# One piece of weights with each of the first four blocks, and the first three FFN products in halves of 256 columns

## The chip, the cores and the metric

The kernel runs on one core of a Trainium2 chip. The metric is the device time of one execution in microseconds (us). Of the core's engines, five matter here: TensorE (PE, matrix products and transposes; PEld is its loading of the stationary operand), VectorE (DVE), ScalarE (ACT), GpSimd (POOL), and SyncE (SP), whose queue issues nearly all DMAs. All arithmetic is in float32; the FFN's weights arrive as float64 and are converted on the chip.

## The reference

A retention attention over 8 batches of 8 heads, 576 positions, head size 64, is followed by a maxout feed-forward network (FFN) over the 4608 resulting rows of 512:

```
scores = q @ k.T / sqrt(64)                      # per batch and head
D[h, i, j] = gamma[h] ** (i - j) if i >= j else 0
attn = (scores * D) @ v                          # (8, 8, 576, 64) -> x (4608, 512)
h = max(max(x @ w1, x @ w2), x @ w3)             # w1, w2, w3: 512 x 768
out = h @ w_out                                  # w_out: 768 x 512
```

## The kernel before

**Tiles.** The 4608 rows are cut into blocks of 128 (`C`) and tiles of 512 (`NT`, so four blocks, `CPT`). The FFN works on a whole tile: `ffn(t)` for tile t, while the attention of tile t+1 is worked in between (`steps`, L1058). Only tile 0 has no earlier FFN to lie beside: its four blocks are worked ahead of and inside the first products. That opening is what the change touches.

**A block's attention.** `load(g)` (L248) issues the DMAs of k, q and v of block g on SP's queue, 256 KB each. `transposes` (L278) turns k and q on TensorE into PSUM, and ScalarE copies each out (`kT`, `qT`, L299). `scores(g)` (L301) makes the score products (L313, tile s) and their mask on VectorE (L336), and returns a function `state` that makes the key-value sums (L318, in the same PSUM tiles as the scores) and the running state on VectorE (L344 to L350). The key-value sums need v scaled by `decay` (L264): on GpSimd for blocks 1 and 2, on VectorE for blocks 0 and 3. `values([g])` (L429) makes masked scores times v (L454) and adds the part of the older state (L445); one-column copies called `first` on VectorE (L458) stand between. It returns a function, called `output` where it is used, that adds the second part and writes x, transposed, to `xT` on VectorE (L224).

**The FFN's products.** A unit is a pair of column blocks `fb` of one weight matrix `i`; `w(i, fb)` is one piece of weights, 512 x 128 float64 values, 512 KB, loaded by `load_weights` (L535) with two DMAs. `up_plain(t, h, fb, i, *parts)` (L870) makes one product of 512 columns in PSUM (four steps of depth 128), in parts if `parts` names ends: the first part is issued at once, and functions for the others and for the last step are returned. The last step is a ScalarE copy for i = 0 (L882) and a VectorE maximum otherwise (L880). Units 0 to 2 are i = 0, 1, 2 for `fb` 0 and 1.

**Conversion.** `convert_all` (L701) is one list of steps, taken a few at a time by `convert(n)` (L819). A piece goes through: exponent (VectorE L717, ScalarE `mant` L719), fraction (ScalarE L725, VectorE L726, ScalarE L728), whole (VectorE L731), sign and product (VectorE L735, L743, the converted piece w). The first six pieces go singly, later ones in pairs. After a product, the next piece not yet loaded is loaded.

**Order.** Each engine's instructions stand in the order of the program text, written out by hand, so where a `convert` stands decides what waits behind what on VectorE and ScalarE. `warm(n, ident)` (L173) issues n matmuls of 128 columns that compute nothing that is used. PSUM has three rings of buffers: `ps_r` (four), `ps_x` and `ps_y` (two each); a buffer is taken again when its last readers are through. The opening's order stands in L1010 to L1056 and goes on in `first_ups` (L889), which `ffn(0)` calls for unit 0.

Of the kernel before, what the change touches and what calls it, by code (L numbers as in the profile page):

```python
# [98 lines left out]
def kernel(  # L99
# [329 lines left out]
    def values(chunks):  # L429
        chore(len(urgent))  # L430
        t, i = divmod(chunks[0], CPT)
        return (chunk_values if chunks[0] >= BY_CHUNKS else parity_values)(chunks, t, i)

    def parity_values(chunks, t, i):
        pool, tag = (ps_r, "r") if chunks[0] >= CPT - 1 else (ps_y, "y")
        o = [pool.tile([P, len(chunks), NP, D], FP32, tag=tag, name="o") for _ in range(2)]
        cross = ((0, 0), (1, 1), (0, 1), (1, 0))

        def old(n):
            for b, g in enumerate(chunks):  # L440
                for u in range(0, NP, 2):
                    for j, c in cross:
                        m = j ^ n
                        if place(g, m) > 0:
                            nc.tensor.matmul(o[m][half(c), b, u + j, :],  # L445
                                             lhsT=(mids if m else states)[g][half(j), head(c, u) // 2, :],
                                             rhs=qks[g]["q"][half(j), head(c, u) // 2, half(m)],
                                             start=False, stop=True, skip_group_check=True)

        for b, g in enumerate(chunks):  # L450
            for u in range(NP):
                for m, c in cross:
                    h = head(c, u)
                    nc.tensor.matmul(o[m][half(c), b, u, :], lhsT=vds[g][half(m), h, :], rhs=sts[g][half(m), h, :],  # L454
                                     start=b == 0 and u == 0, stop=place(g, m) == 0, skip_group_check=True)
        old(0)
        for m in range(2):
            (nc.vector.tensor_copy if t == 0 else nc.scalar.copy)(first[:], o[m][:, 0, 0, 0:1])  # L458

        def rest():  # L460
            old(1)
            if t == 0:
                chunk_output(o, chunks, t, i)
            else:
                between.append(partial(chunk_output, o, chunks, t, i))

        if t == 0:
            return rest
        between.append(rest)
# [349 lines left out]
    def convert(n):  # L819
        for _ in range(n):  # L820
            next(converting, None)
# [67 lines left out]
    def first_ups(h):  # L889

        g = CPT - 1
        rest0, last0, copy0 = up_plain(0, h, 0, 0, 2 * C, g * C)
        transposes(g, "k")
        state()
        output = values([2])
        transposes(g, "q")
        convert(1)
        output()
        convert(1)
        following = scores(g)  # L900
        rest0()
        last1, copy1 = up_plain(0, h, 1, 0, g * C)
        convert(2)
        decay(g)
        following()
        output = values([g])
        convert(1)
        output()
        convert(1)
        for step in (last0, copy0, last1, copy1):  # L910
            step()
        convert(6)

    def ffn(t):

        h = hpool.tile([P, NF, NT], FP32, tag="h", name="h")
        if t == 0:
            a, b, c, d = range(CPT, 2 * CPT)
            middles = {units[2]: [(transposes, a)], units[3]: [(scores, a)], units[5]: [(scores, b)],
                       units[8]: [(scores, c, d)]}  # L920
            for fp, i in units:
                if (fp, i) == units[0]:
                    first_ups(h)
                    yield
                    continue
                for fb in (2 * fp, 2 * fp + 1):
                    maximum, = up_plain(t, h, fb, i)
                    if (fp, i) == units[-1] and fb % 2:
                        maximum()
                        convert(2)  # L930
                    else:
                        convert(4 if (fp, i) == units[1] else 2)
                        maximum()
                    for step, *blocks in middles.get((fp, i), ()) if fb == 2 * fp else ():
                        for g in blocks:
                            step(g)
                    scale(3)
                    if between:
                        between.pop()()
                yield  # L940
            convert(3)
            for fb, _ in enumerate(downs_plain(t, h, range(NF // 2))):
                convert(4 * len(pieces) if fb else 2)
                scale(4)
                if fb == 1:
                    while_converting.close()
                    late["pool"] = ctx.enter_context(tc.tile_pool(name="late", bufs=1))
                    state_factors()
                    nc.gpsimd.tensor_copy(causal[half(1), 0:D], causal[half(1), half(1)])
                    late_room()  # L950
                    weight_sums(0)
                if fb == 2:
                    between.pop()()
                chore((0, 2, 6, 6, len(chores), 0)[fb])
                if fb == 3:
                    between.pop()()
                if fb in (1, 3):
                    yield
            yield
            return  # L960
        order = (0, 2, 1)
        if t == 1:
            spread.append(True)
            weight_sums(2)
            weight_sums(1)
            form_groups = seven_forms(order)
        if t == 2:
            out_sums(order)
        total = len(order) * 2 * len(PRODUCTS)
        count = parts = 0  # L970
        for fp in order:
            while fp not in summed_fp:
                chore()
            for step, _ in enumerate(up(t, h, fp)):
                if step % 4 == 1 or step % 4 == 3 and len(urgent) > (2 if t == 1 else 6):
                    chore(len(urgent) > 0)
                elif chores:
                    chores.popleft()()
                if step % 3 == 2:
                    scale()  # L980
                if t == 1 and fp == order[-1] and step == 19:
                    chores.extend(form_groups[0])
                count += 1
                if count * (NF // 2 * 3) >= (parts + 1) * total:
                    parts += 1
                    yield
            if t == 1:
                seven_hidden(h, fp)
            elif fp != order[-1]:
                chores.extend(sums_of_hidden(h, order, 3 - order.index(fp)))  # L990
        chore(len(urgent) + len(chores))
        if t == 1:
            for n, _ in enumerate(downs_seven(t, order)):
                if n == 0:
                    for step in form_groups[1]:
                        step()
                chore(4)
                scale(2)
                if n in (1, 3):
                    yield  # L1000
        else:
            for n, _ in enumerate(downs(t, h, order)):
                chore(2)
                scale()
                if n in (3, 9):
                    yield
        yield


    warm(6)  # L1010
    load(0)
    load(1)
    load_weights(1)
    load(2, "kq")
    load_weights(1)
    load(2, "v")
    load(CPT - 1, "kq")
    load_weights(1)
    load(CPT - 1, "v")
    load_weights(1)  # L1020
    load_weights(2)
    for b in range(2):
        nc.vector.transpose(columns[b], rows[b])
        for c in range(2):
            shape = [D, 2, 4, 32]
            nc.vector.tensor_copy(
                factors[half(c)].rearrange("p (u b j) s -> p u b j s", b=2, j=4)[:, :, b],
                columns[b][half(c), 8 * c:8 * c + 8].rearrange("p (u j) -> p u j", j=4).unsqueeze(3).to_broadcast(shape))
# [3 lines left out]
    transposes(0)  # L1032
    warm(2)
    decay(1)
    state = scores(0)
    transposes(1, "k")
    state()
    transposes(1, "q")
    output = values([0])
    state = scores(1)  # L1040
    output()
    state()
    convert(2)
    warm(3, ident)
    output = values([1])
    warm(3, ident)
    output()
    transposes(2, "k")
    convert(1)
    warm(2, ident)  # L1050
    transposes(2, "q")
    convert(1)
    decay(2)
    warm(4, ident)
    state = scores(2)
    convert(2)  # L1056

    def steps(t):  # L1058

# [97 lines left out]
```

## Time and profile before

| what | value |
|---|---|
| median of 3 runs (lowest, highest) | 747.76 us (746.92, 749.10) |
| the profiled execution: its own time | 747.25 us |
| its span, first to last instruction | 745.5 us |
| TensorE busy in the span | 736.0 us, 99% |
| VectorE, ScalarE, GpSimd busy | 578.5, 344.8, 34.5 us |
| granted TensorE clock, mean | 0.999 |
| DMA over the span, mean | 79 GB/s |

Of the 40 slices of 18.6 us into which the page cuts the span, the first four move 214 to 263 GB/s: the opening is also when DMA is busiest. In the rows of a timeline the first number is the start in us from the span's start, the second the length in us, then engine, source line, operation, tile written <- tiles read, sizes and count; the bracket gives the idle time ahead of it and what ended that. A count of a product is in records: eight for the four steps of one product or part of it.

### The profile page before, as it was taken

The page shows a single profiled execution, that of the slowest core. Times are in us where ns is not written, and L with a number is a line of the kernel's source. Part 1 is how long each engine was busy: PE and PEld are TensorE (multiplying, and loading weights), DVE is VectorE, ACT ScalarE, POOL GpSimd, SP SyncE. Part 2 cuts the span into 40 slices and gives each one's busy share as a digit, 9 for nine tenths or more (in the row PEclk, how much of TensorE's full clock was granted, in tenths as well). Part 3 has the DMA queues.
Part 4 walks back from the last instruction along what each step waited for, and adds up shares of the span by engine and source line. Part 5 has one row for each costly group of instructions (what it writes and reads, how often), then busy time and mean ns, then how long its engine had stood idle before and what let it go on. Part 6 is the DMA issues. An engine that isn't in the chain of part 4 may idle for free.

```text
span 745.5 us, 17909 instructions
## 1 busy us (share of the span) xinstructions
PE 736.0 (99%) x7236; PEld 608.0 (82%) x7236; DVE 578.5 (78%) x1081; ACT 344.8 (46%) x731; POOL 34.5 (5%) x40
## 2 busy tenths in 40 slices
PE   8899999999999999999999999999999999999998
PEld 7645555888888888888888888888888888888887
DVE  6699898899886996588668877688668956893676
ACT  4376643555245443545354435552455345424441
POOL 1000000022000000000000001000100010000000
PEclk9999999999999999999999999999999999999999
DMA  9999352504242515242433234141514150001001
GB/s 214 237 234 263 91 99 65 93 18 83 72 88 46 92 35 114 44 77 46 95 70 63 53 71 100 30 87 46 119 27 95 39 113 22 3 23 35 0 1 58
DMA packets 226644, 58.91 MB, mean 79 GB/s; under 512 B 207872, under 2 KB 225280, under 8 KB 226560
## 3 DMA queue, kind: packets, MB, share of 16 engines
q1 hardware_dynamic: 225584, 57.71, 35.7%
q8 instruction: 57, 0.93, 0.5%
q14 instruction: 27, 0.22, 0.1%
q10 hardware_dynamic: 976, 0.04, 0.1%
HBM read 48.27 MB, written 9.44 MB: 77 GB/s over the span
## 4 chain that ended last, share of the span: by engine, by line
PE 95%; DVE 2%; DMA 1%; issue 1%; SPq 0%; ACT 0%; POOL 0%; DVEq 0%
PE a L850 19%; PE b L850 17%; PE c L850 9%; PE up L875 7%; PE di L694 6%; PE d L850 6%; PE e L850 6%; PE dhc L694 5%; PE deg L694 3%; PE sk L386 3%; PE down L862 3%; PE o L481 2%; PE dfd L694 2%; PE o L488 2%; PE dx L601 1%; PE kv L389 1%
## 5 line engine op out<-in xcount | busy, mean ns | idle before, releaser
L838 DVE TENSOR_TENSOR part<-part 128x512 f32<-128x512 f32 x168 | 117.9, 702 | 86.5 <-ACT part L835 83.9
L835 ACT COPY part<-b 128x512 f32<-128x512 f32 x120 | 70.3, 586 | 163.4 <-PE b L850 161.4
L838 DVE TENSOR_TENSOR h<-h,part 128x512 f32<-128x512 f32 x120 | 83.3, 694 | 24.5 <-ACT h L835 20.5
L835 ACT COPY part<-a 128x512 f32<-128x512 f32 x96 | 56.3, 586 | 50.7 <-PE a L850 50.2
L212 ACT ACTIVATE vraw<-vraw,gk 128x64 f32<-128x64 f32 x240 | 76.8, 347 | 0.9 <-DMA vraw<-in_v_dram 0.8
L850 PE MATMUL b<-s,n 128*128 128x256 f32 x288 | 73.9, 379 | 0.0
L875 PE MATMUL up<-xT,w 128*128 128x512 f32 (+3 forms) x168 | 65.1, 538 | 2.3 <-DVE w L743 1.4
L850 PEld LDWEIGHTS b<-s,n 128*128 128x128 f32 x288 | 54.7, 190 | 7.4
L875 PEld LDWEIGHTS up<-xT,w 128*128 128x128 f32 x168 | 29.1, 190 | 31.5 <-issue 25.5
L850 PE MATMUL c<-xT,w 128*128 128x256 f32 x192 | 51.2, 389 | 0.0
L683 ACT COPY k<-di 128x256 f32<-128x256 f32 x49 | 18.2, 372 | 68.5 <-PE di L694 43.4
L850 PE MATMUL d<-s,w 128*128 128x256 f32 x192 | 49.8, 380 | 0.0
L850 PE MATMUL b<-xT,n 128*128 128x256 f32 x192 | 49.3, 379 | 0.0
L850 PE MATMUL a<-s,w 128*128 128x256 f32 x192 | 49.3, 379 | 0.0
L850 PE MATMUL a<-xT,w 128*128 128x256 f32 x192 | 49.3, 379 | 0.0
L403 POOL TENSOR_TENSOR s<-s,gs_of 64x512 f32<-64x512 f32 x21 | 22.5, 1071 | 568.7 <-DVE s L401 534.7
L850 PE MATMUL a<-xT,n 128*128 128x256 f32 x192 | 45.4, 379 | 0.0
L850 PE MATMUL e<-xT,w 128*128 128x256 f32 x192 | 45.4, 379 | 0.0
L850 PEld LDWEIGHTS e<-xT,w 128*128 128x128 f32 x192 | 36.5, 190 | 5.4 <-issue 0.5
L850 PEld LDWEIGHTS a<-xT,w 128*128 128x128 f32 x192 | 36.5, 190 | 5.0
L850 PEld LDWEIGHTS a<-s,w 128*128 128x128 f32 x192 | 36.5, 190 | 5.0
L850 PEld LDWEIGHTS b<-xT,n 128*128 128x128 f32 x192 | 36.5, 190 | 5.0
(191 smaller groups left out, 1385.3 us busy)
## 6 DMA issues: line engine op xcount, KB each, us to landing
bits<-in_moe_w_dram SPq DMA_DIRECT2D x36, 256.0 KB, 5.5
kraw<-in_k_dram SPq DMA_DIRECT2D x32, 256.0 KB, 3.2
vraw<-in_v_dram SPq DMA_DIRECT2D x32, 256.0 KB, 3.6
qraw<-in_q_dram SPq DMA_DIRECT2D x224, 32.0 KB, 2.1
kxraw<-in_k_dram SPq DMA_DIRECT2D x224, 32.0 KB, 2.1
out_dram<-osb SPq DMA_DIRECT2D x56, 128.0 KB, 1.7
bits<-in_moe_w_out_dram SPq DMA_DIRECT2D x6, 512.0 KB, 5.8
qraw<-in_q_dram SPq DMA_DIRECT2D x7, 256.0 KB, 5.7
```

Source lines behind the costliest of these rows:

```text
L212: scaling.popleft()()
L386: nc.tensor.matmul(s[half(c), h, :], lhsT=kT[half(c), h, :], rhs=qT[half(c), h, :], start=True, stop=True)
L403: nc.gpsimd.tensor_tensor(new, new, factor, op=ALU.mult)
L481: nc.tensor.matmul(o[m][half(c), n, u, :], lhsT=vds[g][half(m), h, :], rhs=sts[g][half(m), h, :], start=n == 0 and u == 0, stop=place(g, m ...
L488: nc.tensor.matmul(o[m][half(c), n, u, :], lhsT=stacks[g][half(m), h, :], rhs=qks[g]["q"][half(m), h, :], start=False, stop=True, skip_gro ...
L683: nc.scalar.copy(place, a)
L694: nc.tensor.matmul(banks[chain], lhsT=hidden(h, order, b, late_ones)[:, e], rhs=late["V"][v][:, e], start=begins and e == 0, stop=chain no ...
L835: nc.scalar.copy(of[step], ps[step[0]][:])
L838: nc.vector.tensor_tensor(of[dst], a, b, op=op)
L850: nc.tensor.matmul(ps[chain][:, e, :], lhsT=factor(w, 2 * fp + e), rhs=xS[t][x], start=n == 1 and e == 0, stop=ends, skip_group_check=True)
L862: nc.tensor.matmul(b[:], lhsT=h[:, fb, m * P:(m + 1) * P], rhs=w_sb["out", fb], start=fb == blocks[0], stop=fb == blocks[-1])
L875: nc.tensor.matmul(ps[:, a:b], lhsT=w_sb[i, fb][:, dc * P:(dc + 1) * P], rhs=xT[t][:, dc, a:b], start=dc == 0 and a == 0, stop=dc == NDC - ...
```

## The change

Three things are different in the opening; nothing is changed from unit 1's second product on.

- Loads: one piece of weights is loaded behind each of blocks 0 to 3, and two more at the end. Before, pieces stood behind block 1, inside block 2's loads, inside block 3's and after them.
- The order of the opening: the scores and the key-value sums of blocks 0 and 1 are issued together; block 2's transposes stand at the end of the opening and its scores in `first_ups`; the idle `warm` matmuls with `ident` are 21 where they were 12.
- The first three products (w(0, 0), w(0, 1), w(1, 0)) are each made in two halves of 256 columns: the first halves between the attention of blocks 2 and 3, the second halves after block 3. Before, the first was made in 256 + 128 + 128 columns, the second in 384 + 128, and the third whole in `ffn`, which now skips it. The values of block 2 take their buffers from `ps_r`, not `ps_y`.

```diff
-        pool, tag = (ps_r, "r") if chunks[0] >= CPT - 1 else (ps_y, "y")
+        pool, tag = (ps_r, "r") if chunks[0] >= CPT - 2 else (ps_y, "y")
...
     def first_ups(h):
         g = CPT - 1
-        rest0, last0, copy0 = up_plain(0, h, 0, 0, 2 * C, g * C)
+        rest0, copy0 = up_plain(0, h, 0, 0, 2 * C)
+        convert(1)
+        state = scores(g - 1)
+        convert(1)
+        state()
+        rest1, copy1 = up_plain(0, h, 1, 0, 2 * C)
+        output = values([g - 1])
         transposes(g, "k")
+        output()
+        transposes(g, "q")
+        convert(3)
+        state = scores(g)
+        decay(g)
+        convert(1)
+        rest2, maximum2 = up_plain(0, h, 0, 1, 2 * C)
         state()
-        output = values([2])
-        transposes(g, "q")
-        convert(1)
+        output = values([g])
+        convert(2)
         output()
-        convert(1)
-        following = scores(g)
-        rest0()
-        last1, copy1 = up_plain(0, h, 1, 0, g * C)
         convert(2)
-        decay(g)
-        following()
-        output = values([g])
-        convert(1)
-        output()
-        convert(1)
-        for step in (last0, copy0, last1, copy1):
+        for step in (rest0, copy0, rest1, copy1):
             step()
-        convert(6)
+        convert(2)
+        rest2()
+        convert(4)
+        maximum2()
...
                 for fb in (2 * fp, 2 * fp + 1):
+                    if (fp, i) == units[1] and fb == 0:
+                        continue
...
-    load(0)
-    load(1)
-    load_weights(1)
-    load(2, "kq")
-    load_weights(1)
-    load(2, "v")
-    load(CPT - 1, "kq")
-    load_weights(1)
-    load(CPT - 1, "v")
-    load_weights(1)
+    for g in range(CPT):
+        load(g)
+        load_weights(1)
     load_weights(2)
...
-    state = scores(0)
+    scores(0)()
+    convert(2)
+    output = values([0])
+    warm(4, ident)
+    convert(1)
+    output()
+    warm(4, ident)
     transposes(1, "k")
-    state()
+    warm(3, ident)
     transposes(1, "q")
-    output = values([0])
-    state = scores(1)
-    output()
-    state()
-    convert(2)
+    convert(1)
+    warm(4, ident)
+    scores(1)()
     warm(3, ident)
     output = values([1])
     warm(3, ident)
     output()
-    transposes(2, "k")
-    convert(1)
-    warm(2, ident)
-    transposes(2, "q")
-    convert(1)
+    transposes(2)
+    convert(2)
     decay(2)
-    warm(4, ident)
-    state = scores(2)
-    convert(2)
```

## The prediction

> **What bounds the kernel now.** I read the page's shares first, then the chain, then the waits of TensorE in two stretches, then each engine's timeline up to 110 us. Below: the span, TensorE's busy row, and the chain by engine.
>
> ```profile
> span 745.5 us, 17909 instructions
> PE 736.0 (99%) x7236; PEld 608.0 (82%) x7236; DVE 578.5 (78%) x1081; ACT 344.8 (46%) x731; POOL 34.5 (5%) x40
> ...
> PE 95%; DVE 2%; DMA 1%; issue 1%; SPq 0%; ACT 0%; POOL 0%; DVEq 0%
> ```
>
> TensorE sets the end, and asked for its waits from 55 us on the trace names none over 0.2 us. From there the program is the same list of instructions before and after, so the change is worth what it does to the moment at which TensorE goes dense; a delay there is paid once and not won back. Up to 55 us TensorE does wait:
>
> ```profile
> PE up L875 <- DVE w L743: 1.4, 3, 0.7
> PE o L445 <- DVE first L458: 1.1, 2, 0.9
> ...
> PE s L318 <- POOL vd L273: 0.9, 1, 0.9
> PE up L875 <- DVE xT L224: 0.9, 1, 0.9
> ```
>
> (total us, times, longest.) It waits for converted weights, for the state steps of a block, and for the last block's x. Its timeline (start, length) there:
>
> ```profile
> 15.71 0.65 PE L298 MATMUL kt<-ident,kraw 128*128 128x128 f32 x4
> ...
> 18.97 1.99 PE L875 MATMUL up<-xT,w 128*128 128x256 f32 x8
> ...
> 24.28 1.06 PE L313 MATMUL s<-qT,kT 64*64 64x64 f32 x32
> ...
> 26.63 2.82 PE L875 MATMUL up<-xT,w 128*128 128x384 f32 x8 [0.20 <-DVE w L743]
> 29.38 0.69 PE L318 MATMUL s<-vd,kraw 64*64 64x64 f32 x32
> ...
> 33.27 5.49 PE L875 MATMUL up<-xT,w 128*128 128x128 f32 x24 [0.88 <-DVE xT L224]
> 39.48 7.13 PE L875 MATMUL up<-xT,w 128*128 128x512 f32 x16 [0.72 <-DVE w L743]
> ```
>
> Note where the attention of blocks 2 and 3 runs: block 2 is transposed at 15.7, block 3 scored at 24.3 and its key-value sums made at 29.4, all before the conversion of the third piece of weights is done. Last, the two ScalarE rows that decide the after:
>
> ```profile
> 17.56 0.59 ACT L299 COPY qT<-qt 128x512 f32<-128x512 f32 x1 [0.57 <-PE qt L298]
> 18.04 0.77 ACT L719 ACTIVATE mant<-bits,one 128x512 f32<-128x512 uint32 x1
> ```
>
> The second piece's ScalarE step starts when the copy written ahead of it is through, not when its bytes land (16.9: issued 12.4, 4.5 to land).
>
> **What the Trainium skill says.** "TensorE: Matmul & The Clock Gate", on engine queue depths in Part 1: ScalarE and VectorE take their instructions strictly in order. The two rows above agree. The same page, Part 1 (the HAM clock gate): about 3.4 us of idleness halves TensorE's clock. The trace agrees on there being a slow state: the first warming matmuls take 244 ns a record (2.93 us for 12), later ones 130; afterwards its longest wait before is 0.9 us, so no re-throttling is shown. "PSUM — Partial Sum Buffer", PSUM bank collisions: two engines must not touch one bank and quadrant at once, so guard by bank. The trace doesn't contradict: block 0's key-value sums, in the bank its masks read, start at 7.93, the masks end at 7.95 (the clash is only with the last mask's bank).
>
> **The method.** I walked both programs along each engine's order: an instruction starts when the one before it on its engine is through its slot and its inputs are there. Slots from before's timelines: transposes 0.46, scores 0.60, key-value sums 0.50, values 0.47, warm(4) 0.98-1.04, a 256-column half 1.83, a whole product 3.54; ScalarE copy 0.49, mantissa 0.66, the two exponent steps 0.74 and 0.63; VectorE mask pair 0.67, state steps 1.33, x pair 0.67, conversion steps 0.34, 0.34, 0.61, 0.72, 0.61. For the kernel before this gives the second product of unit 1 at 39.0 (trace 39.48) and the first of unit 4 at 60.3 (trace 60.67).
>
> **Loads.** Same DMAs, other order on SP's queue, at about 1.1-1.3 us per 256 KB. Before, positions land at 4.0, 5.0, 6.2, 7.2, 8.1, 10.6, 11.5, 12.9, 13.5, 14.6, 15.6, 16.9, 18.3, 19.0, 20.0, 21.3, 22.4, 23.4 (issue plus landing of each). Reassigned: piece 0 at 8.3 (was 12.9), k, q, v of block 1 at 10.3, 11.5, 12.8 (7.2, 8.1, 10.6), piece 1 at 14.6, block 2 at 15.6 to 18.3, piece 2 at 20.2, block 3 at 21.3 to 23.4. In the walk each is wanted later: k of block 1 at 12.3, v at 15.6 (its POOL step of 1.05 ends at 13.9, the sums start at 16.6), piece 0 at 10.0, piece 1 at 20.7, k of block 3 at 28.6. So the reorder costs nothing; 2 us later for everything would cost 0.4, 3 us 1.4. Later pieces wait for buffers freed by conversion steps, so SP's queue shifts with the rest.
>
> **Blocks 0 and 1.** Scores and key-value sums of a block are now issued together, so the sums wait for the masks' bank: 0.9 us for block 0 (7.95), 0.9 for block 1. Warm matmuls (ident) rise from 12 to 21, nine more at 0.245: 2.2 us, mostly on the path because TensorE's queue is what moves block 1 on. kt1 12.3, qt1 13.6 (its PSUM buffer, third in a ring of two with the warms, waits for the kT copy), scores 15.1, sums 16.6, values 17.9, x of block 1 20.0-20.8 (was 16.5). Block 2's transposes: 19.9, was 15.7, **+4.2**.
>
> **First halves.** First product's 256 columns at 21.2 (was 19.0), scores of block 2 behind it at 23.0 (was 18.3). The second piece's mantissa step stands behind qT2's copy: 21.5; exponents to 23.7; sign and product on VectorE follow mask 2: weights at 25.9, was 26.5. So the piece that landed 2.3 us earlier is ready 0.6 earlier. TensorE idles 0.8 for it; second half-product 25.9-27.7.
>
> **Block 3.** Values of block 2 come behind that, at 27.7 (21.8 before), then kt3 28.6, qt3 29.4, scores 30.7 (24.3 before). The third piece's mantissa step is written after qT3's copy: 30.6; exponents to 32.7; mask, decay, sign, product on VectorE: weights at 34.7 (34.5 before). Its half-product is issued ahead of block 3's key-value sums, so these, which need nothing of it, wait: TensorE idles 3.4 us, runs the half 34.7-36.6, and the sums start at 36.6 (29.4 before), **+7.2**. State steps, first, two conversion steps, x of block 3: 40.4 (33.2 before), +7.2.
>
> **After block 3.** Left before unit 1's second product: three halves, 5.5 us, to 45.9; before 5.5 (33.27 to 38.8) plus 0.72 of waiting for weights, 39.5: +6.4. Before waits 0.5 more at 51.44 for the next pair's weights; after, these are done at 56.9, 0.6 before they are wanted: +5.9. The walk of before falls 0.4 short of its trace, in gaps of 0.1-0.2 that show as "issue" around transposes; with the like in the after, +6.4, as the difference of the two walks says (66.7 against 60.3). Splitting costs nothing in itself: six halves 11.0, and before 1.83+2.72+3 x 1.05+3.54 = 11.2. The pool of the values (ps_r) costs nothing: its banks' last readers, xT of block 2 and kT3, qT3, are through before TensorE comes. The skipped product and the conversion count (22 by the same point) only move.
>
> **Sum.** Profiled execution 747.25 (span 745.5, 1.75 around it) + 6.4 = 753.7; the median shown, 747.76, is 0.5 above it: 754.2, +0.9%. About 0.3% (2.2 us) is what can be told from no change.
>
> **Rivals.** (B) The key-value sums don't wait for the masks, the dependency being kept by columns and not by bank: blocks 0 and 1 each 0.9 sooner, +4.6, 752.4. Against it the PSUM page; the 7.93 start is not decisive. (C) The clock: from 27.7 to 34.7 TensorE has only 2.9 us of small matmuls, then 3.4 idle. If it drops to half, up to one window of 3.4 us of work runs at half speed, 1.7 lost, at most two: +8 to +10, about 756. Lower bound nothing. (N) Not slower: the pieces landing early are converted early, so TensorE never waits for weights. Landed at 14.6 and 20.2, plus 4.6 from exponent to product (13.96 to 18.53 for piece 0), they would be there at 19.2 and 24.8; then the three waits on weights, 1.4 us, go: 747.76 - 1.4 = 746.4. It decides if piece 2's mantissa step can start 3.4 us earlier, by 27.2; the written order, after qT3, speaks against it. Without any warm matmuls both walks still differ by 4.8, so those alone don't turn the sign.
>
> **Chances.** Forecast 0.62 (752.8 to 755.5), B 0.16 (751 to 752.8), C 0.14, N 0.08 (half of it or more within 0.3%). Range 751.0 to 758.0: it takes in B and nearly all of C, and leaves out N. Faster 0.03, same 0.05, slower 0.92.
>
> **What would show it.** Right: kt of block 2 near 20, second weights near 26, key-value sums of block 3 behind the third half near 36.6 after an idle of over 3 us with DVE w named, x of block 3 near 40.4, no TensorE wait past 46. B: block 1's sums directly behind its scores. C: the eight records of a 256-column half taking over 3 us, not 2, after 34.7. Wrong: the third weights before 32, or TensorE waits after 55 that before lacks.

## The result and the profile after

The changed kernel takes 758.07 us (median of 4 runs, 755.53 to 759.04); the kernel before, beside it, 748.09 us. The ratio is 1.0129, with a 95% interval of 1.0099 to 1.0158: slower by 1.3%. The profiled execution of the changed kernel is the fastest of the four, 755.53 us, with a span of 753.8 us where before has 745.5: +8.3 us.

These answer to the lines shown of before: the span, the busy times and the chain by engine, from the page of the changed kernel.

```profile
span 753.8 us, 17948 instructions
PE 740.3 (98%) x7254; PEld 613.2 (81%) x7254; DVE 578.5 (77%) x1081; ACT 344.6 (46%) x731; POOL 34.6 (5%) x40
...
PE 97%; DVE 1%; ACT 1%; ACTq 0%; issue 0%; DVEq 0%
```

TensorE is busy 4.3 us longer and waits 4.0 us longer. Asked for TensorE's waits from 60 us on, the trace again names none: all of it is in the opening. Its waits up to 60 us (total us, times, longest):

```profile
PE up L875 <- DVE w L743: 3.9, 2, 3.3
PE s L318 <- DVE m L336: 1.8, 3, 0.6
PE o L445 <- DVE first L458: 1.3, 2, 0.9
...
PE up L875 <- DVE xT L224: 0.9, 1, 0.9
```

One wait for converted weights is now 3.3 us long. The wait of key-value sums for the masks is new, three times 0.6 us. TensorE's timeline (start, length) shows where they lie:

```profile
20.50 0.66 PE L298 MATMUL kt<-ident,kraw 128*128 128x128 f32 x4
...
21.83 1.99 PE L875 MATMUL up<-xT,w 128*128 128x256 f32 x8 [0.24 <-ACT kT L299]
...
26.64 1.99 PE L875 MATMUL up<-xT,w 128*128 128x256 f32 x8 [0.64 <-DVE w L743]
...
31.74 0.69 PE L313 MATMUL s<-qT,kT 64*64 64x64 f32 x32 [0.67 <-ACT qT L299]
35.72 3.68 PE L875 MATMUL up<-xT,w 128*128 128x256 f32 x8 [3.29 <-DVE w L743]
39.33 0.69 PE L318 MATMUL s<-vd,kraw 64*64 64x64 f32 x32
...
43.25 12.31 PE L875 MATMUL up<-xT,w 128*128 128x256 f32 x40 [0.91 <-DVE xT L224]
```

Block 2 is transposed at 20.5 (15.7 before), block 3 scored at 31.7 (24.3) and summed at 39.3 (29.4), and its x lets TensorE go at 43.25 (33.27). Compare the three half-products: the first two take 1.99 us, the third, after the idle of 3.3 us, takes 3.68 for the same eight records. The windows view says why. Its columns are the stretch, its length, busy time and count of PE, PEld, DVE, ACT and POOL, then the granted TensorE clock, the DMA share and GB/s.

```profile
32.00:36.00 4.00, 0.71 (x33) 0.57 (x23) 3.25 (x6) 2.33 (x4) 0.00 (x0) 0.98 0.88 219
36.00:40.00 4.00, 4.00 (x52) 2.79 (x55) 0.00 (x0) 0.00 (x0) 0.00 (x0) 0.59 1.00 233
40.00:44.00 4.00, 2.22 (x71) 1.78 (x61) 3.68 (x11) 1.44 (x2) 0.00 (x0) 1.00 0.02 4
44.00:48.00 4.00, 4.00 (x20) 3.53 (x19) 2.47 (x6) 1.58 (x3) 0.00 (x0) 1.00 0.52 134
```

TensorE was busy 0.71 of 4 us, and the clock then stood at half for about 3.4 us; 1.7 us were lost. So the loss has two parts: work that comes later in the written order, and a clock that falls in the hole this leaves. The timed runs seem to differ mainly in the second: their mean clocks were 0.998, 0.995, 0.995 and 0.993, their spans 753.8, 756.1, 757.3 and 756.6 us. As an estimate, the span times what the mean clock lacks of 1.0 is 1.5, 3.8, 3.8 and 5.3 us; less that, the spans are 751.3 to 753.5.

ScalarE's timeline has the step on which the hole hangs, the third piece's mantissa step, directly behind the copy of block 3's qT:

```profile
31.10 0.59 ACT L299 COPY qT<-qt 128x512 f32<-128x512 f32 x1 [0.40 <-PE qt L298]
31.58 0.77 ACT L719 ACTIVATE mant<-bits,one 128x512 f32<-128x512 uint32 x1
```

Behind it VectorE still has block 3's masks (0.67 us) and the scaling of its v (0.60) ahead of the piece's last two steps.

### The profile page after: what moved, and what is told of

It reads as the page before. It is cut to its first block, busy times and chain, and to the rows that moved or that the text cites. A ratio compares the mean times of both kernels' runs of the same rounds, so it can differ in the third digit from the quotient of the medians.

```text
span 753.8 us, 17948 instructions
## 1 busy us (share of the span) xinstructions
PE 740.3 (98%) x7254; PEld 613.2 (81%) x7254; DVE 578.5 (77%) x1081; ACT 344.6 (46%) x731; POOL 34.6 (5%) x40
## 4 chain that ended last, share of the span: by engine, by line
PE 97%; DVE 1%; ACT 1%; ACTq 0%; issue 0%; DVEq 0%
PE a L850 19%; PE b L850 16%; PE c L850 9%; PE up L875 9%; PE di L694 6%; PE d L850 6%; PE e L850 5%; PE dhc L694 5%; PE deg L694 3%; PE sk L386 3%; PE down L862 3%; PE o L481 2%; PE dfd L694 2%; PE o L488 2%; PE dx L601 1%; PE kv L389 1%
## 5 line engine op out<-in xcount | busy, mean ns | idle before, releaser
L838 DVE TENSOR_TENSOR h<-h,part 128x512 f32<-128x512 f32 x120 | 83.3, 694 | 24.6 <-ACT h L835 20.5
L875 PE MATMUL up<-xT,w 128*128 128x512 f32 (+1 forms) x168 | 66.4, 548 | 5.1 <-DVE w L743 3.9
L875 PEld LDWEIGHTS up<-xT,w 128*128 128x128 f32 x168 | 31.9, 195 | 32.7 <-issue 25.0
L683 ACT COPY k<-di 128x256 f32<-128x256 f32 x49 | 18.3, 373 | 68.5 <-PE di L694 42.1
L850 PEld LDWEIGHTS a<-xT,n 128*128 128x128 f32 x192 | 36.5, 190 | 5.0
```

The source lines that it names most:

```text
L683: nc.scalar.copy(place, a)
L838: nc.vector.tensor_tensor(of[dst], a, b, op=op)
L850: nc.tensor.matmul(ps[chain][:, e, :], lhsT=factor(w, 2 * fp + e), rhs=xS[t][x], start=n == 1 and e == 0, stop=ends, skip_group_check=True)
L875: nc.tensor.matmul(ps[:, a:b], lhsT=w_sb[i, fb][:, dc * P:(dc + 1) * P], rhs=xT[t][:, dc, a:b], start=dc == 0 and a == 0, stop=dc == NDC - ...
```

## The experiments

Each ran beside the kernel before on the same chip, in three sets: the first four, the next four, the last two. Where a mean clock is given beside a span it tells two causes apart: a run with a clock of 1.0 has lost next to nothing to the clock. In the first set the kernel before had five such runs with spans of 745.0 to 746.7 us (mean 746.0), six at 0.998 with 746.9 to 748.4, and one at 0.991 with 754.4: it loses clock too. Runs at 1.0 still differ, those of before in the last set by 2.7 us, so a mean of two or three of them is good to about 1 us.

**Filling the hole.**

```diff
+        filler = ps_y.tile([P, P], FP32, tag="y", name="warm")
+        for _ in range(12):
+            nc.tensor.matmul(filler[:], lhsT=ident[:], rhs=ident[:], start=True, stop=True)
         rest2, maximum2 = up_plain(0, h, 0, 1, 2 * C)
```

> The changed kernel, with twelve 128-column matmuls that compute nothing put on TensorE's queue ahead of the third product's first half, where it idles 3.3 us for the converted weights. Order theory (6.4 to 6.8 us of the loss are later attention in the written order, the rest is the clock falling to half in that idle): the half takes 2.0 us again and not 3.68, the mean clock is 0.998 or more, the span is about 752.1 (753.8 less 1.7), the time about 754 and its spread under 1.5 us; still 5.5 to 7 us over the kernel before. Clock rival (the idle and what follows from it is the whole loss): the time falls to within 2 us of before, 748 to 750. Rival that the clock has no part: nothing moves, about 758.

Measured: 754.49 us (754.34 to 755.96), ratio 1.0084 (1.0069 to 1.0100). The clock is 1.0 in three of five runs, with spans of 752.6 to 752.7. Its TensorE timeline, from the filling on:

```profile
33.01 2.94 PE L908 MATMUL warm<-ident 128*128 128x128 f32 x24
36.38 1.99 PE L875 MATMUL up<-xT,w 128*128 128x256 f32 x8 [0.43 <-DVE w L743]
38.31 0.69 PE L318 MATMUL s<-vd,kraw 64*64 64x64 f32 x32
```

The half is back at 1.99 us, though it starts 0.7 later than in the changed kernel's profile. So the clock is worth 758.07 - 754.49 = 3.6 us between the medians of two sets (4.2 when each is taken against the kernel before beside it), and 752.7 - 746.0 = 6.7 us remain with the clock full. The filling does not always keep it full: the other two runs are at 0.998 and 0.997. Both the clock rival and the view that the clock has no part fall.

**The third product whole, after block 3.**

```diff
-        rest2, maximum2 = up_plain(0, h, 0, 1, 2 * C)
         state()
...
             step()
-        convert(2)
-        rest2()
-        convert(4)
+        maximum2, = up_plain(0, h, 0, 1)
+        convert(6)
         maximum2()
```

> The changed kernel, with the third product made whole after block 3 rather than in two halves around it. Order theory: the key-value sums of block 3 no longer stand behind weights that are not converted; they start near 34.4, where its scaled v is done, and not at 39.3; x of block 3 is done near 38.5 (43.2); but 1.8 us of product move behind it, so of the walk's 6.4 only 1.0 comes back, and the clock's 1.7 or more: span about 751, time about 753 (+5). Rival (putting the half ahead of block 3's sums is the main loss): x of block 3 at 36 or earlier and a time of 750 or less.

Measured: 754.62 us (754.18 to 755.6), ratio 1.0083 (1.0068 to 1.0097). TensorE's timeline:

```profile
34.71 1.13 PE L318 MATMUL s<-vd,kraw 64*64 64x64 f32 x32 [1.97 <-DVE vd L273]
...
39.27 16.36 PE L875 MATMUL up<-xT,w 128*128 128x256 f32 x40 [0.88 <-DVE xT L224]
```

The sums start 4.6 us sooner than in the changed kernel, now held by block 3's scaled v, and x of block 3 is there 4.0 sooner. But 1.8 us of product come behind it, and the clock still falls: at half from about 34 to 44 us (0.993 in the profile, 0.993 to 0.995 in the others). The fall begins only 1.1 us into the wait of 1.97. The time is 1.6 us over what was expected. In the profile x of block 3 is 0.8 later than expected, and the 40 records take 16.36 us where, by the prediction's slots, two halves and three whole products come to 14.3: the clock is most of it. The order in which it happened was as expected.

**The third piece converted ahead.**

```diff
         rest1, copy1 = up_plain(0, h, 1, 0, 2 * C)
+        convert(3)
         output = values([g - 1])
         transposes(g, "k")
         output()
         transposes(g, "q")
-        convert(3)
+        convert(1)
         state = scores(g)
         decay(g)
-        convert(1)
         rest2, maximum2 = up_plain(0, h, 0, 1, 2 * C)
```

> The changed kernel, with the third piece's first three conversion steps taken ahead of block 2's values and block 3's transposes, so that its ScalarE step is not behind the copies of kT and qT; sign and product follow block 2's output. Order theory: the mantissa step starts near 25 (31.6), the weights are ready near 32.6 (35.7), TensorE's idle of 3.3 us goes and with it the clock's fall; x of block 3 near 38.4; span about 749 (3.1 less than the walk gave, and no clock loss), time 750.5 to 751.5, still +2.5 to +3.5. Rival (late conversion is not what holds the half, the bytes are): the weights stay at 35 or later and the time at 757 or more.

Measured: 752.9 us (751.45 to 753.27), ratio 1.0052 (1.0038 to 1.0066). TensorE's timeline:

```profile
32.93 1.99 PE L875 MATMUL up<-xT,w 128*128 128x256 f32 x8 [0.24 <-DVE w L743]
34.85 0.69 PE L318 MATMUL s<-vd,kraw 64*64 64x64 f32 x32
...
38.76 13.98 PE L875 MATMUL up<-xT,w 128*128 128x256 f32 x40 [0.91 <-DVE xT L224]
```

The edit moves three steps ahead of block 2's values and of block 3's two copies, and the last step (sign and product) ahead of block 3's masks and scaled v. The wait goes from 3.29 to 0.24 us, and 5.2 us of the median come back. That shows the place of the conversion in the written order, not the arrival of the bytes, to be what held the half. (ScalarE's copies and VectorE's masks are passed in one edit, so their shares aren't told apart.) Two runs at clock 1.0 have spans of 749.7 and 749.9, +3.8 over before (walk: +3.3). The four others lost 1.5 us to the clock, which is why the time is above the 751.5 expected; it fell although TensorE's longest wait after the start is 0.91 us:

```profile
36.00:37.00 1.00, 0.53 (x18) 0.32 (x14) 0.86 (x4) 0.00 (x0) 0.00 (x0) 1.00 1.11 316
37.00:38.00 1.00, 0.46 (x16) 0.32 (x16) 0.90 (x6) 0.26 (x1) 0.00 (x0) 1.00 0.88 192
38.00:38.70 0.70, 0.00 (x0) 0.00 (x0) 0.70 (x4) 0.67 (x2) 0.00 (x0) 1.00 0.92 237
38.70:40.00 1.30, 1.24 (x3) 1.06 (x4) 1.27 (x4) 0.52 (x1) 0.00 (x0) 0.52 1.05 283
```

From 36.0 to 38.7 TensorE is busy 1.0 of 2.7 us, around block 3's output, and then runs at half speed. But that stretch is not enough for a fall: the changed kernel has it too (40.5 to 43.2, 1.0 of 2.7 us busy), and so has the kernel before (30.5 to 33.3, 1.05 of 2.8), and in both of these profiles the clock behind it stays at 1.00.

**The first products as before, the rest as changed.** Here `first_ups`, the third product in `ffn` and the buffers of block 2's values are those of the kernel before, behind the changed loads and opening (the scores of block 2 come after `decay(2)`). Part of the edit, against the changed kernel:

```diff
     decay(2)
+    state = scores(2)
...
-                    if (fp, i) == units[1] and fb == 0:
-                        continue
```

> The changed kernel's loads and opening, with first_ups, the skipped product and the buffers of block 2's values as before. Order theory: block 2's transposes stay near 20.3, but block 3 is scored near 28 and summed near 33 (31.7 and 39.3 changed, 24.3 and 29.4 before), x of block 3 near 36; no idle over 1.5 us, full clock; the walk gives +3.6: time 751 to 752.5. Rival (the halves are the whole loss): within 1.5 us of before.

Measured: 752.18 us (751.45 to 753.5), ratio 1.0046 (1.0031 to 1.0060); at clock 1.0 spans of 749.7 to 751.0, mean 750.2, +4.2 over before. In its timeline block 2's transposes start at 21.23, block 3's scores at 28.98, its sums at 34.08, and TensorE goes on with x of block 3 at 37.96. These starts are 0.9 to 2.0 us later than expected; the time is as expected. The loss that is in the opening alone is there, and nothing of the 3 us hole. Two of the six runs still lost clock.

**The opening and the loads as before, the first products as changed.** Part of the edit, against the changed kernel:

```diff
-    for g in range(CPT):
-        load(g)
-        load_weights(1)
+    load(0)
+    load(1)
+    load_weights(1)
...
-    scores(0)()
-    convert(2)
-    output = values([0])
+    state = scores(0)
+    transposes(1, "k")
+    state()
...
```

> The kernel before's loads and opening (12 warm matmuls, state sums apart from the scores) with the changed first_ups, skipped product and buffers. Order theory: block 2's transposes near 15.7, block 3 scored near 28 and summed behind the third half near 34, x of block 3 near 37; the walk gives +3.3 with the clock full, and the idle ahead of the third half is still over 3 us, so the clock can fall and cost 1.5 to 3.5 more: time 752 to 755. Loads rival (the order of loads and the opening are the whole loss): within 1 us of before.

Measured: 753.51 us (752.91 to 755.74), ratio 1.0074 (1.0050 to 1.0097). No run kept the clock full; the three at 0.998 have spans of 751.2 to 752.0, which less 1.5 us (0.002 of the span) is about +4. Block 2 is transposed at 16.14, block 3 scored at 29.71; the half starts after a wait of 3.04 us at 33.69 and takes 3.78. The time is in the range expected, the order slower: block 3's scores, its sums (37.41) and its x (41.76) are 1.7, 3.4 and 4.8 us later than expected, 1.8 us of that the half at its slow clock. So each part of the change costs about 4 us by itself, and the two don't add (6.7 together). The timeline says where they overlap: block 2 is transposed 4.4 us sooner than in the changed kernel, but the first half then waits 0.97 us for its weights and starts at 19.83, only 2.0 sooner. The new buffers of block 2's values were never tried alone; in the changed kernel these values start as the second half ends (28.56), with no wait named.

**The loads alone.** The changed order of loads in the kernel before (the first four lines of the diff above, the other way round).

> The kernel before with the changed order of loads alone. The prediction's sum took the reorder as free in the changed order of work. In the old order it is not covered: block 1's k is wanted at 7.4 and lands at 9.8, its v at 13.6 and not 10.6, so its key-value sums start near 14.8 and not 11.9 and everything behind them is 3.0 late: time +3, near 751. If loads are free anywhere: within 1 us of before.

Measured: 752.67 us (750.02 to 756.01, 12 runs), ratio 1.0051 (1.0033 to 1.0070). Its timeline has the wait:

```profile
9.77 0.63 PE L298 MATMUL kt<-ident,kraw 128*128 128x128 f32 x4 [2.69 <-DMA kraw<-in_k_dram]
```

The one run at full clock has a span of 748.3, +2.3 (3.0 by the walk); the others are up to 6 us longer, with clocks of 0.990 to 0.998. In the profile it is at half from 12 to 16 us and again around 32 to 35. The median is 1.7 us over the 751 expected. In the old order of work the loads' order is not free.

**The old loads in the changed kernel.** The same lines, put back in the changed kernel.

> The changed kernel with the old order of loads. If the changed order of loads were what makes it slow, this would be faster than the changed kernel. Order theory: the opposite. Piece 0 lands at 12.9 and not 9.4, and its exponent step on VectorE now stands ahead of block 0's output copies, so block 0's second sums, block 1's transposes and all behind wait: block 2's transposes near 23 (20.5), 2.9 us later than the changed kernel, span about 755.5 with the clock full, time 757 to 761.

Measured: 761.69 us (760.33 to 763.43), ratio 1.0179 (1.0153 to 1.0204): slower than the changed kernel, in another set, by about 3.6 us, and just past the expected end. Its clocks are lower too (0.989 to 0.993). Block 2 is transposed at 25.56, 2.6 later than expected; the clock, at 0.53 to 0.61 from 12 to 20 us, is likely part of that. The changed order of loads fits the changed order of work; it isn't what makes it slow.

**No warm matmuls.** The changed kernel without `warm(…, ident)` in the opening.

> The changed kernel without the opening's 21 ident warm matmuls. The walk gives 2.3 us back: block 2's transposes near 18, span with the clock full about 750.4 (+4.1). But without them TensorE's work up to 22 us is thin, so if the clock falls there too, small matmuls run at half speed and the idle ahead of the third half is as long: mean clock 0.993 or lower and a time of 752.5 to 757. If the warm matmuls were the whole loss: 749 or less.

Measured: 758.61 us (757.74 to 759.11), ratio 1.0135 (1.0115 to 1.0155), clock 0.984 to 0.989: above the expected end and level with the changed kernel. The clock is at half from 12 to 24 us, so block 2's transposes start at 20.07 and not near 18. In the medians the 21 warm matmuls pay for themselves and no more. What they cost with the clock full isn't shown, since no run without them kept it.

**Two versions of the kernel before.** The fourth piece's exponent and fraction ahead of the copies of h, and the same with three filling matmuls ahead of and behind block 3's output. The diff is that of the second.

```diff
         output = values([g])
         convert(1)
+        filler = ps_y.tile([P, P], FP32, tag="y", name="warm")
+        for _ in range(3):
+            nc.tensor.matmul(filler[:], lhsT=ident[:], rhs=ident[:], start=True, stop=True)
         output()
+        for _ in range(3):
+            nc.tensor.matmul(filler[:], lhsT=ident[:], rhs=ident[:], start=True, stop=True)
         convert(1)
+        convert(2)
         for step in (last0, copy0, last1, copy1):
             step()
-        convert(6)
+        convert(4)
```

> The kernel before with the fourth piece's exponent and fraction steps taken ahead of the first two products' last parts, so that its ScalarE steps do not stand behind the two copies of h. The same walk gives 1.3 us less: the waits of 0.72 and 0.52 us for weights at 39.5 and 51.4 go. Time 746.5 to 747.5 against before in the same call; with the rival that these waits are replaced by others, no change.

> The same, with three filling matmuls of 128 columns in each of the two waits of 0.9 us around block 3's output. If the clock falls in part of the runs because TensorE's work is thin from 29.4 to 33.2, the share of runs with a mean clock under 0.999 goes down and the median falls by up to 1 us more, to 745.5 to 747; the filling itself (0.73 us each) fits into the waits. If the clock falls for another reason: as the run without filling.

Measured: without filling 746.78 us (22 runs), ratio 0.9980 (0.9973 to 0.9986); with it 746.27 us (8 runs), ratio 0.9974 (0.9963 to 0.9984), beside 748.38 us of before. Both waits for weights, of 0.72 and 0.52 us, are gone: from 30 to 60 us the unfilled version's trace names only the two waits of 0.9 us around block 3's output, and the filled one's none. TensorE's timeline of the filled version:

```profile
31.62 0.94 PE L910 MATMUL warm<-ident 128*128 128x128 f32 x6
32.55 0.46 PE L445 MATMUL o<-qT,state 64*64 64x64 f32 x16
32.95 0.94 PE L913 MATMUL warm<-ident 128*128 128x128 f32 x6
33.89 12.35 PE L875 MATMUL up<-xT,w 128*128 128x128 f32 x40
```

All eight filled runs have a clock of 1.0; unfilled, six of 22 are at 0.998 or below. (The unfilled profile, at clock 1.0, has the second longest span of its set, 746.1; 1.69 us of that is a gap inside block 1's values that the trace calls "issue" and the filled profile lacks.) The two medians differ by 0.5 us with intervals that overlap, so the filling's own share isn't settled. The filled version beats both kernels, by 2.1 us and, across sets, by about 12.

## Why the prediction was right, and where it was not

**The bound.** Right: after the opening TensorE has no wait in either kernel, and a delay of the opening is paid once.

**Loads.** Right in effect. Piece 0 was put at 8.3 and landed at 9.4, block 1's k at 10.3 (9.8), its v at 12.8 (13.6); all before they were wanted. That the cover counts is shown by the loads-only kernel: +2.3 us in its one run at full clock, with nothing else moved.

**Blocks 0 and 1.** Right, +4.2 predicted for block 2's transposes and +4.8 measured. The sums do wait for the masks (1.8 us in three waits), so rival B, +4.6, falls. The nine warm matmuls more were counted as a cost of 2.2 us. The run without any shows the other side: taking them all away gains nothing, and the clock falls. How the opening's loss splits between them and the sums' waits stays open.

**First halves and block 3.** Right in mechanism and nearly in size. Predicted and measured starts: first half 21.2 and 21.83, second weights' end 25.9 and 26.58, block 3's scores 30.7 and 31.74, third weights 34.7 and 35.67. The differences grow slowly to 1.0 us, partly since a half's slot is 1.92 us and not 1.83; the walk of before was itself 0.4 to 0.5 short. The second piece was to be ready 0.6 sooner than before; it is ready at 26.58, and in before's trace at 26.48, so its earlier landing gained nothing. With the clock full the predicted +6.4 is +6.7 (filled run).

**The clock.** This is the step that failed: rival C was put at 0.14 as the alternative to the forecast, whose own sum gave the clock nothing, and it came on top of it in all four runs. Its size was given as 1.7 for one window and at most two; the profile lost 1.7, and the other three, estimated from their mean clocks, two to three times that. The filled run gives 3.6 us in the median. The prediction foresaw an idle of 3.4 us (3.3 measured), as long as the idle after which, by the Trainium skill ("TensorE: Matmul & The Clock Gate", Part 1), the clock halves, and it gave no reason for leaving the fall out. The runs agree that such an idle can end in a fall, but the length is no threshold here. With the third product whole the clock is at half 1.1 us into a wait of 2.0, and with the third piece converted ahead it falls with no wait over 0.91 us. Nor is the busy share one: of the changed kernel's windows of 4 us, the one with 0.7 us busy (32 to 36) was followed by a fall, and those with 2.2 (40 to 44) and 2.7 (24 to 28) were not. The slow start that the prediction took for the slow state isn't in the clock column either, which reads 1.00 from 0 to 4 us.

**Sign and size.** 754.2 was predicted and 758.07 measured, against a before of 747.76 and 748.09: +6.4 against +10.0 us. The 3.6 missing are of the size of what the filling returns, 3.6 to 4.2. The median lies at the very end of the stated range (751.0 to 758.0), which reached so far only because it took in rival C; the forecast's own part of it ended at 755.5.

**Rival N** fell in the kernel as changed, but its mechanism is real: the run that moves the third piece's steps forward recovers 5.2 us. It isn't enough to turn the sign: that run is still 4.2 us slower than before.

Open is what sets off the clock's fall, since the same stretch of work is followed by one in some profiles and not in others, and why it costs more in one run than in another; runs of one kernel differ in both.

## What to carry to other kernels

In an opening where each engine takes its work in the written order, ask of each conversion step which copy or mask stands ahead of it, and of each product which work that doesn't need it stands behind it: bytes that land earlier help only as far as the step that uses them is written earlier. A product put into a gap ahead of the last block's attention delays all that waits for that block. Where a reordering thins out a stretch of TensorE's work, allow for a loss by the clock on top of the one worked out, and test for it by filling the hole: here neither the longest idle nor the busy share told which stretch would bring it.

## What the runs showed that I had not expected

The clock can fall without a long wait: 1.0 busy of 2.7 us was followed by half speed with no idle over 0.91 us, and yet other profiles have this stretch at a full clock. The fall lasts some 3.4 us (38.7 to about 42.1) or several times that (about 34 to 44 with the third product whole). Twelve filling matmuls that compute nothing, put where TensorE waits anyway, gave 3.6 us. Most kernels' runs hold more than one mean clock, the kernel before's too, so its part of a few us is seen only where the clock of each run is read beside its span.
